# Value product of a pooled attention with 128-row operands in place of 48-row ones

## The chip, the cores and the metric

The kernel runs on one core of a Trainium2 chip. The metric is the device time of one execution in microseconds, from launch to end; the median of several runs stands for a kernel. One execution was recorded by the hardware profiler, and its span, from the first to the last instruction, is the profiled time.

## What is computed

An attention with pooled keys and values, and behind it two layers of a feed-forward network, in float32.

```python
# q, k, v: (8 batches, 8 heads, 576 tokens, 64)
k_p = k.reshape(B, H, 72, 8, D).mean(axis=3)      # 576 keys -> 72
v_p = v.reshape(B, H, 72, 8, D).mean(axis=3)
attn = softmax(q @ k_p.T / sqrt(D))
x = (attn @ v_p) as (4608 tokens, 512)
h = x @ moe_w_in;   x = piecewise(h) @ moe_w_out  # 512 -> 2048 -> 512
h = x @ moe2_w_in;  out = (h - tanh(h)) @ moe2_w_out
```

## The kernel before, in words

The 4608 tokens are cut into twelve blocks of 384 (`TB`). The first layer runs over all blocks, then the second, and each block takes 16 steps, one for each 128 of the 2048 inner features. A step `t` is twelve products of 384 columns (`h_mm`, the tile `ph`) and twelve for step `t - 2` (`out_mm`, tiles `po`). A float32 product of full accuracy is made of three products of two halves each: an operand is cut into `hi`, a `float32r` number, and `lo`, the rest.

The attention of block `j` runs between the steps of the block ahead of it, one pair of heads (`p`) in four steps. A pair of heads has 2 x 72 = 144 pooled keys: 128 of them, the main part, fill a tile's rows, and 16 are left over. These 16 make the 48 rows of this change: the value side `vr` has the `hi` values, then their `lo` part, then `hi` again, 16 rows each, and the attention side `ar` the matching rows, so that one product gives the three terms for the 16 keys.

Block 0's attention and the conversion of the first weights come ahead of the first step (`startup`); during the first 14 steps the weights of the first layer are converted from float64 on ScalarE, VectorE and GpSimd (`w1_prep`, `conv`). A table of step numbers (`plan`) says in which step each piece of attention is issued, and a scheduler in the building program then orders the instructions of each engine.

The functions that matter here:

- `constants` clears `kvraw`'s third part on GpSimd and makes the identity `ident`.
- `kv_pool` sums eight neighbouring keys and values on GpSimd into `bd`: `bd[:, 0]` and `bd[:, 1]` are the 128 main keys and values, `bd[:, 2]` the 16 left over, copied to several rows, the keys' at rows 64 to 79.
- `kv_v` (lines 224 to 234) makes `vh`, `vl` and the 48-row `vr` on VectorE. `vr` comes from a pool of five tiles.
- `kv_k_pe` (236 to 241) turns the keys on TensorE, the main ones by a 128-row transpose (`L239`), the 16 by a 16-row one (`L240`), into one PSUM tile `pkt`.
- `softmax_b` writes the normalised attention and takes a tile `ar` of 48 rows from a pool with one place; `at_pe` turns it; `at_evac` copies the result into `ar`, rows 0 to 31 on ScalarE, rows 32 to 47 on VectorE.
- `pv` (382 to 394) is the value product: four products into one PSUM tile, `vh`, `vl`, `vr`, `vh` against attention (`L390` to `L393`). A block that lies in two batches has two pieces of 192 columns, others one of 384.

Of the kernel before, what the change touches and what calls it, by code (L numbers as in the profile page):

```python
# [17 lines left out]

# Float32 products at float32 accuracy: every operand is cut exactly into
# hi = float32r(x) and lo = x - hi, and a*b is hi*hi + hi*lo + lo*hi.  # L20
#
# The weights come in as float64. A pair of 32-bit words becomes the nearest float32:
# taken as a float32, the upper word has the exponent's upper eight bits as its exponent,
# so that times 2**-112 moves the exponent's bias by 896, from float64's to float32's
# (what is too small becomes 0). The bits then move up by three, the lower word's upper
# three bits, rounded, are added, and the sign is put back.
REBIAS = 2.0**-112
# [3 lines left out]
def attention_two_moe_kernel(  # L31
# [11 lines left out]
    nc = tc.nc  # L43
# [34 lines left out]

# [1 line left out]
    kvraw = const.tile([P, 3, POOL * D], F32, tag="kvraw", name="kvraw")  # L80
    ident = const.tile([P, P], F32, tag="ident", name="ident")
    half = const.tile([P, 1], F32, tag="half", name="half")
    mask = const.tile([P, 2], F32, tag="mask", name="mask")
    nsel = const.tile([P, 1], F32, tag="nsel", name="nsel")

    def constants(sel):
        nc.gpsimd.memset(kvraw[:, 2, :], 0.0)
        make_identity(nc, ident)
        nc.vector.memset(half, 0.5)
        nc.vector.memset(nsel, 0.0)  # L90
        nc.vector.memset(nsel[32:48], -1.0)
        nc.vector.tensor_reduce(mask[:, 0:1], ident[:, 0:SP], AX.X, ALU.add)
        nc.vector.tensor_reduce(mask[:, 1:2], ident[:, SP:P], AX.X, ALU.add)
        nc.vector.tensor_scalar(mask, mask, 1.0 / POOL, None, ALU.mult)
        nc.vector.memset(sel, 0.0)
        nc.vector.tensor_scalar(sel[:, SP : 2 * SP], ident[0:SP, 0:SP], 1.0 / POOL, None, ALU.mult)
        for c in range(3):
            o = 3 * SP + c * NR
            nc.vector.tensor_scalar(sel[:, o : o + NR], ident[0:SP, SP - NR : SP], 1.0 / POOL, None, ALU.mult)

# [1 line left out]
    WI = [None] * FC  # L102
# [30 lines left out]
    def w1_prep(f):  # L133
        r = raws.pop((0, f))
        if f + 1 < FC - 1:
            # the room that the next weights will have
            a, s = w_slot(f + 1, "l", I32, "wf"), w_slot(f + 1, "h", I32, "ws")
        else:
            a, s = staging(), r[..., 0]
        conv(r, a, s)  # L140
        hi, lo = (w_slot(f, x, F32R, f"w{x}") for x in "hl")
        a = a.bitcast(F32)
        nc.scalar.activation(hi, a, AF.Copy)  # L143
        for io, eng in ((0, nc.vector), (1, nc.gpsimd)):
            eng.tensor_tensor(lo[:, io], a[:, io], hi[:, io].bitcast(F32), ALU.subtract)  # L145
            (WI, WO)[io][f] = (hi[:, io], lo[:, io])
# [16 lines left out]

# [1 line left out]
    xt = {}  # L165
# [21 lines left out]
    def pieces(j):  # L187
        """(first token in block, tokens, batch, first token in batch)"""
        done, res = 0, []
        while done < TB:  # L190
            b, s = divmod(j * TB + done, S)
            n = min(TB - done, S - s)
            res.append((done, n, b, s))
            done += n
        return res
# [8 lines left out]
    def tree(eng, a):  # L204
        """sums of the POOL parts of the last axis, left in its first part"""
        n = POOL * D // 2
# [4 lines left out]
    def kv_pool(b, p):  # L211
# [7 lines left out]
        eng.tensor_scalar(bd[:, 2, D : 2 * D], kvraw[:, 2, 0:D], 1.0 / POOL, None, ALU.mult)  # L219
        r = slice(HP, HP + NR)  # L220
        U[("k", b, p)] = (bd[:, 0], bd[r, 2], ident[r, r])
        U[("v", b, p)] = (bd[:, 1], bd[0:48, 2])

    def kv_v(b, p):
        main, rem = U.pop(("v", b, p))
        vh = kvp.tile([P, P], F32R, tag="vh", name="vh")
        vl = kvp.tile([P, P], F32R, tag="vl", name="vl")
        vr = kvp.tile([48, P], F32R, tag="vr", name="vr")
        vx = at.tile([48, P], F32R, tag="vx", name="vx")
        nc.vector.tensor_copy(vh, main)  # L230
        nc.vector.tensor_copy(vx, rem)
        nc.vector.tensor_tensor(vl, main, vh.bitcast(F32), ALU.subtract)
        nc.vector.scalar_tensor_tensor(vr, vx.bitcast(F32), nsel[0:48], rem, ALU.mult, ALU.add)
        vt[(b, p)] = (vh, vl, vr)

    def kv_k_pe(b, p):
        main, rem, idr = U.pop(("k", b, p))
        ps = ps_a.tile([P, 2 * SP], F32, tag="pa", name="pkt")
        nc.tensor.transpose(ps[:, 0:P], main, ident)  # L239
        nc.tensor.transpose(ps[:, P : 2 * SP], rem, idr)  # L240
        U[("pkt", b, p)] = ps
# [54 lines left out]
    def parts(j):  # L296
        """(batch, tile of tokens in the block, first token in the tile, tokens)"""
        if j == 1:
# [32 lines left out]
    def softmax_b(j, p, eng):  # L331
# [11 lines left out]
        if n == 3:  # L343
            eng.tensor_copy(rr[:, :, 2], px)
        ar = at.tile([48, TB], F32R, tag="ar", name="ar")
        U[("pr", j, p)] = (pn, rr, ar)

    def at_pe(j, p):
        pn, rr, ar = U.pop(("pr", j, p))
        pm = p_tile(j, [P, TB], "pam")  # L350
# [7 lines left out]
        else:  # L358
            pr = ps_a.tile([96, P], F32, tag="pa", name="par")
            nc.tensor.transpose(pr, rr.rearrange("t i c s -> t (i c s)").bitcast(F32), ident)  # L360
        U[("pm", j, p)] = (pm, pr, ar)

    def at_evac(j, p):
        pm, pr, ar = U.pop(("pm", j, p))
        ah = a_tile(j, [P, TB], F32R, "ah")
        al = a_tile(j, [P, TB], F32R, "al")
        if j < 2:
            nc.scalar.activation(ah, pm, AF.Copy)
            nc.vector.tensor_tensor(al, pm, ah.bitcast(F32), ALU.subtract)
            nc.scalar.activation(ar, pr, AF.Copy)  # L370
        else:
            for i in range(NTI):
                c = slice(i * P, (i + 1) * P)
                nc.scalar.activation(ar[0:32, c], pr[32 * i : 32 * i + 32], AF.Copy)
                nc.vector.tensor_copy(ar[32:48, c], pr[32 * i : 32 * i + NR])
            nc.scalar.activation(ah, pm, AF.Copy)
            nc.vector.tensor_tensor(al, pm, ah.bitcast(F32), ALU.subtract)
        U[("at", j, p)] = (ah, al, ar)

    def pv(j, p):  # L380
        ah, al, ar = U.pop(("at", j, p))
        ps = p_tile(j, [P, TB], "ppv")
        for off, n, b, s in pieces(j):
            vh, vl, vr = vt[(b, p)]
            if j == 1:
                t = slice(b * HP, (b + 1) * HP)
                o, xh, xr, xl = (x.rearrange("p (i t) -> p i t", t=P)[:, :, t] for x in (ps, ah, ar, al))
            else:
                o, xh, xr, xl = (x[:, off : off + n] for x in (ps, ah, ar, al))
            nc.tensor.matmul(o, vh, xh, start=True, stop=False)  # L390
# [10 lines left out]

# [1 line left out]
    hp = {}  # L403
# [93 lines left out]

# [1 line left out]
    def startup(used):  # L499
# [88 lines left out]

# [1 line left out]
    plan = {}  # L590
# [8 lines left out]
    def ahead(kind, fn, a):  # L599
        """Queue a load; each is issued when a buffer of its kind has been used."""  # L600
        loads[kind].append((fn, a))
# [119 lines left out]
```

## Time and profile before

| | us |
|---|---|
| median of 3 runs | 1824.53 |
| lowest, highest | 1823.83, 1825.07 |
| span of the profiled execution | 1822.8 |
| TensorE busy | 1782.7 (98%) |
| VectorE busy | 942.8 (52%) |
| ScalarE busy | 726.7 (40%) |
| GpSimd busy | 292.3 (16%) |

TensorE's products overlap: a product of 384 columns is shown as 0.34 us long while the next starts half that later. What it costs on the queue is therefore read from the distance of two starts. A float32 product that is no transpose is two passes in the trace, and each has a record of its own.

### The profile page before, as it was taken

The numbers are of one execution on the slowest core, as the hardware profiler recorded it, in microseconds if no ns is written. First come the engines' busy times: TensorE is split into PE (matmuls) and PEld (weight loads), VectorE is DVE, ScalarE is ACT, GpSimd is POOL, SyncE is SP. The second block draws the span as 40 slices with busy tenths as digits, with TensorE's granted clock in tenths as the row PEclk, the third lists the DMA queues.
The fourth block names the chain that finished last, engine by engine and source line by source line (L and its number), as shares of the span: only waits on it lengthen the run. The fifth ranks groups of instructions, "written<-read, shape, count | busy, mean of one in ns | idle before, by whom it ended". The sixth has DMA issues, their size and how long they took to land.

```text
span 1822.8 us, 25870 instructions
## 1 busy us (share of the span) xinstructions
PE 1782.7 (98%) x9616; PEld 1654.3 (91%) x9616; DVE 942.8 (52%) x1841; ACT 726.7 (40%) x1849; POOL 292.3 (16%) x382
## 2 busy tenths in 40 slices
PE   6888999999999999999999999999999999999999
PEld 4778999999999999999999999999999999999998
DVE  6898676766677666665556432332332332332222
ACT  4665554544444454443445432332232322332222
POOL 4695133320332202320100000000000000000000
PEclk8899999999999999999999999999999999999999
DMA  6462233413323232320114210110110010010000
GB/s 176 162 185 79 78 91 87 115 39 94 94 74 97 71 96 61 83 56 10 27 47 127 81 35 1 35 35 1 35 35 1 35 35 18 18 35 18 18 18 18
DMA packets 129133, 110.47 MB, mean 61 GB/s; under 512 B 71280, under 2 KB 102000, under 8 KB 129008
## 3 DMA queue, kind: packets, MB, share of 16 engines
q1 hardware_dynamic: 129008, 108.83, 20.0%
q8 instruction: 75, 1.23, 0.3%
q14 instruction: 50, 0.41, 0.1%
HBM read 81.53 MB, written 27.26 MB: 60 GB/s over the span
## 4 chain that ended last, share of the span: by engine, by line
PE 92%; DVE 3%; POOL 1%; DMA 1%; issue 1%; ACT 0%; SPq 0%; DVEq 0%; ACTq 0%; POOLq 0%
PE ph L416 43%; PE po L466 35%; PE pox L466 7%; PE psc L314 2%; PE ppv L392 1%; PE ppv L393 1%; DMA wraw<-in_moe_w_out_dram 1%; PE pam L352 1%; DVE ws L121 1%; PE ppv L390 0%; PE ppv L391 0%; DVE wl L145 0%; DMA kvs<-in_k_dram 0%; POOL wl L145 0%; POOL kvraw L208 0%
## 5 line engine op out<-in xcount | busy, mean ns | idle before, releaser
L416 PE MATMUL ph<-xh,wh 128*128 128x384 f32 x1536 | 524.3, 342 | 2.2 <-ACT wh L143 2.0
L416 PE MATMUL ph<-xh,wl 128*128 128x384 f32 x1536 | 519.3, 338 | 5.5 <-DVE wl L145 5.3
L416 PE MATMUL ph<-xl,wh 128*128 128x384 f32 x1536 | 517.5, 337 | 0.3 <-DVE xl L400 0.3
L433 DVE TENSOR_TENSOR g<-ph,g 128x384 f32<-128x384 f32 x384 | 213.5, 556 | 412.2 <-ACT g L427 315.5
L441 DVE TENSOR_TENSOR gl<-g,gh 128x384 fp32r<-128x384 f32 x369 | 233.7, 633 | 297.6 <-ACT gh L439 296.0
L439 ACT ACTIVATE gh<-g 128x384 fp32r<-128x384 f32 x384 | 200.9, 523 | 333.2 <-PE po L466 185.1
L416 PEld LDWEIGHTS ph<-xh,wh 128*128 128x128 f32 x1536 | 289.3, 188 | 13.7 <-ACT wh L143 2.6
L416 PEld LDWEIGHTS ph<-xl,wh 128*128 128x128 f32 x1536 | 290.0, 189 | 9.0 <-DVE xl L400 0.6
L416 PEld LDWEIGHTS ph<-xh,wl 128*128 128x128 f32 x1536 | 289.8, 189 | 7.7 <-DVE wl L145 7.6
L466 PE MATMUL po<-gh,wh 128*128 128x384 f32 x768 | 262.4, 342 | 0.0
L466 PE MATMUL po<-gl,wh 128*128 128x384 f32 x768 | 258.7, 337 | 1.9 <-POOL gl L441 1.9
L466 PE MATMUL po<-gh,wl 128*128 128x384 f32 x768 | 258.5, 337 | 0.0
L427 ACT ACTIVATE g<-ph 128x384 f32<-128x384 f32 x192 | 94.2, 491 | 325.8 <-PE ph L416 325.8
L425 ACT ACTIVATE g<-g,half 128x384 f32<-128x384 f32 x192 | 118.3, 616 | 163.8 <-DVE g L424 163.5
L466 PE MATMUL po<-wh,gl 128*128 128x512 f32 x384 | 151.9, 396 | 0.0
L466 PE MATMUL po<-wl,gh 128*128 128x512 f32 x384 | 151.7, 395 | 0.0
L466 PE MATMUL po<-wh,gh 128*128 128x512 f32 x384 | 150.3, 391 | 0.0
L466 PEld LDWEIGHTS po<-gl,wh 128*128 128x128 f32 x768 | 145.1, 189 | 2.8 <-POOL gl L441 2.8
L466 PEld LDWEIGHTS po<-gh,wl 128*128 128x128 f32 x768 | 145.1, 189 | 0.0
L466 PEld LDWEIGHTS po<-gh,wh 128*128 128x128 f32 x768 | 145.0, 189 | 0.0
L424 DVE TENSOR_SCALAR g<-ph 128x384 f32<-128x384 f32 x192 | 106.3, 554 | 65.2 <-PE ph L416 61.8
L208 POOL TENSOR_TENSOR kvraw<-kvraw 128x768 f32<-128x768 f32 (+2 forms) x84 | 108.2, 1288 | 109.8 <-DMA kvraw<-in_v_dram 89.4
(119 smaller groups left out, 1953.8 us busy)
## 6 DMA issues: line engine op xcount, KB each, us to landing
wraw<-in_moe_w_in_dram SPq DMA_DIRECT2D x32, 512.0 KB, 4.0
wraw<-in_moe_w_out_dram SPq DMA_DIRECT2D x32, 512.0 KB, 4.7
x2d<-ost SPq DMA_DIRECT2D x48, 192.0 KB, 1.9
xl<-x2d SPq DMA_DIRECT2D x12, 768.0 KB
out_dram<-ost SPq DMA_DIRECT2D x36, 256.0 KB, 2.0
w2d<-wf SPq DMA_DIRECT2D x32, 256.0 KB, 2.3
wl<-w2d SPq DMA_DIRECT2D x32, 256.0 KB, 2.6
kvraw<-in_k_dram SPq DMA_DIRECT2D x28, 256.0 KB, 2.7
```

Of the source, the lines that this page charges most:

```text
L121: nc.vector.scalar_tensor_tensor(s, hw, -0x80000000, s, ALU.bitwise_and, ALU.bitwise_or)
L208: eng.tensor_tensor(a[..., 0:n], a[..., 0:n], a[..., n : 2 * n], ALU.add)
L314: nc.tensor.matmul(ps[t : t + m, i], qt[:, c], kt[(b, p)], start=True, stop=True)
L352: nc.tensor.transpose(pm[:, i * P : (i + 1) * P], pn[:, i, 0:P], ident)
L416: nc.tensor.matmul(ps, a[:, cs], x[:, c, :], start=(i == 0), stop=(i == 3 * KC - 1))
L424: nc.vector.tensor_scalar(a, hp[t], -1.0, 1.0, ALU.max, ALU.min)
L425: nc.scalar.activation(a, a, AF.Square, bias=half, scale=0.5)
L427: nc.scalar.activation(a, hp[t], AF.Tanh)
L433: nc.vector.tensor_tensor(a, hp.pop(t), a, ALU.subtract if ph else ALU.max)
L439: nc.scalar.activation(gh, a, AF.Copy)
L441: eng.tensor_tensor(gl, a, gh.bitcast(F32), ALU.subtract)
L466: nc.tensor.matmul(o, a, m, start=(f == 0 and i == 0), stop=(f == FC - 1 and i == 2))
```

## The change

The tile `vr` becomes one of six tiles of 128 rows that live through the whole kernel, used in turn, and `ar` one of two such tiles, by the parity of `p`. All eight are cleared once on GpSimd in `constants`, and later writes touch rows 0 to 47 alone, so rows 48 to 127 stay zero. The third value product takes all 128 rows. The 16 left-over keys are no longer turned by a 16-row transpose: all 128 rows of `bd[:, 2]` stand as the stationary operand against 16 columns of the identity, those of rows 64 to 79, in an ordinary float32 product. Comments are dropped.

```diff
+    vrs = [const.tile([P, P], F32R, tag=f"vr{i}", name=f"vr{i}") for i in range(6)]
+    ars = [const.tile([P, TB], F32R, tag=f"ar{i}", name=f"ar{i}") for i in range(2)]
+    n_vr = itertools.count()
...
         nc.vector.memset(nsel[32:48], -1.0)
+        for t in (*vrs, *ars):
+            nc.gpsimd.memset(t.bitcast(F32), 0.0)
...
-        r = slice(HP, HP + NR)
-        U[("k", b, p)] = (bd[:, 0], bd[r, 2], ident[r, r])
+        U[("k", b, p)] = (bd[:, 0], bd[:, 2])
...
-        vr = kvp.tile([48, P], F32R, tag="vr", name="vr")
+        vr = vrs[next(n_vr) % len(vrs)]
...
-        nc.vector.scalar_tensor_tensor(vr, vx.bitcast(F32), nsel[0:48], rem, ALU.mult, ALU.add)
+        nc.vector.scalar_tensor_tensor(vr[0:48], vx.bitcast(F32), nsel[0:48], rem, ALU.mult, ALU.add)
...
-        nc.tensor.transpose(ps[:, P : 2 * SP], rem, idr)
+        nc.tensor.matmul(ps[:, P : 2 * SP], rem, ident[:, HP : HP + NR], start=True, stop=True)
...
-        ar = at.tile([48, TB], F32R, tag="ar", name="ar")
...
+        ar_t = ars[p % 2]
...
-            nc.scalar.activation(ar, pr, AF.Copy)
+            nc.scalar.activation(ar_t[0:48], pr, AF.Copy)
...
-                nc.scalar.activation(ar[0:32, c], pr[32 * i : 32 * i + 32], AF.Copy)
-                nc.vector.tensor_copy(ar[32:48, c], pr[32 * i : 32 * i + NR])
+                nc.scalar.activation(ar_t[0:32, c], pr[32 * i : 32 * i + 32], AF.Copy)
+                nc.vector.tensor_copy(ar_t[32:48, c], pr[32 * i : 32 * i + NR])
...
-                o, xh, xr, xl = (x[:, off : off + n] for x in (ps, ah, ar, al))
+                o, xh, xr, xl = (x[:, off : off + n] for x in (ps, ah, ar_t, al))
```

The scheduler orders the first part of the program anew. On GpSimd, at the very start, the program before clears `kvraw`, the identity and a part of `bd`, and goes on to the sums of block 0's values (`kvs`):

```order
L87 MEMSET kvraw 128x512
masks.py:197 MEMSET ident 128x128
L218 MEMSET bd 128x64
masks.py:199 ISA
masks.py:199 AFFINE_SELECT ident<-ident 128x128
L517 TENSOR_TENSOR kvs<-kvs 72x2x256
```

and now, on the same engine at the same place:

```order
masks.py:197 MEMSET ident 128x128
L99 MEMSET vr_130 128x128
masks.py:199 ISA
masks.py:199 AFFINE_SELECT ident<-ident 128x128
L99 MEMSET vr_131 128x128
L99 MEMSET vr_132 128x128
L99 MEMSET vr_133 128x128
L99 MEMSET vr_134 128x128
L99 MEMSET vr_135 128x128
L99 MEMSET ar_136 128x384
L99 MEMSET ar_137 128x384
L226 MEMSET bd 128x64
```

One of the eight new clearings stands ahead of the identity's last step, the other seven behind it and ahead of the first value sum.

On TensorE in block 0's attention (`pq` are the turned queries, `psc` the scores, `pv` the pooled values of the last head pairs) the order was:

```order
L314 MATMUL psc<-kt,qt 128x144 x3
L542 MATMUL pv_382<-vp,sel 128x64
L543 MATMUL pv_382<-vp,sel 48x64
L280 MATMUL pq_421<-ident,qn 64x128 x3
L278 MATMUL pq_421<-ident,qn 64x128 x3
L314 MATMUL psc<-kt,qt 128x144 x3
L390 MATMUL ppv<-ah,vh 128x384
L391 MATMUL ppv<-ah,vl 128x384
L392 MATMUL ppv<-ar,vr 128x384
L393 MATMUL ppv<-al,vh 128x384
```

and is now:

```order
L321 MATMUL psc<-kt,qt 128x144 x3
L550 MATMUL pv_394<-vp,sel 128x64
L551 MATMUL pv_394<-vp,sel 48x64
L398 MATMUL ppv<-ah,vh 128x384
L399 MATMUL ppv<-ah,vl 128x384
L400 MATMUL ppv<-ar_136,vr_130 128x384
L401 MATMUL ppv<-al,vh 128x384
L287 MATMUL pq_432<-ident,qn 64x128 x3
L285 MATMUL pq_432<-ident,qn 64x128 x3
L321 MATMUL psc<-kt,qt 128x144 x3
```

The first value product has moved ahead of the last pair's queries and scores.

On SyncE's queue, where batch 1's keys and values for the second head pair (`kvraw`) are loaded among the weights (`wraw`), the order was:

```order
L200 DMA kvraw<-in_k_dram 128x512
L202 DMA kvraw<-in_k_dram 16x512
L200 DMA kvraw<-in_v_dram 128x512
L110 DMA wraw<-in_moe_w_in_dram 128x4x256
L114 DMA wraw<-in_moe_w_out_dram 128x1024
L202 DMA kvraw<-in_v_dram 16x512
L110 DMA wraw<-in_moe_w_in_dram 128x4x256
L114 DMA wraw<-in_moe_w_out_dram 128x1024
L202 DMA kvraw<-in_v_dram 16x512 x2
```

and is now:

```order
L208 DMA kvraw<-in_k_dram 128x512
L210 DMA kvraw<-in_k_dram 16x512
L118 DMA wraw<-in_moe_w_in_dram 128x4x256
L122 DMA wraw<-in_moe_w_out_dram 128x1024
L208 DMA kvraw<-in_v_dram 128x512
L210 DMA kvraw<-in_v_dram 16x512
L118 DMA wraw<-in_moe_w_in_dram 128x4x256
L122 DMA wraw<-in_moe_w_out_dram 128x1024
L210 DMA kvraw<-in_v_dram 16x512 x2
```

The 128 main rows of the values went behind a pair of weight loads; the last two loads of the same tile stand where they stood.

## Rows read from the trace of the kernel before

**Rows 1.** Page, chain that ended last: share of the span by engine.

```profile
PE 92%; DVE 3%; POOL 1%; DMA 1%; issue 1%; ACT 0%; SPq 0%; DVEq 0%; ACTq 0%; POOLq 0%
```

**Rows 2.** Windows: busy us per engine (instructions), then granted TensorE clock, DMA share, GB/s.

```profile
40.00:60.00 20.00, 16.96 (x55) 12.55 (x55) 17.76 (x33) 10.26 (x19) 9.12 (x8) 0.59 0.40 136
0.00:156.00 156.00, 119.87 (x614) 98.37 (x615) 133.19 (x217) 94.36 (x210) 107.09 (x99) 0.92 0.53 161
156.00:960.00 804.00, 803.66 (x4645) 773.31 (x4645) 527.01 (x1115) 375.94 (x1131) 185.20 (x284) 1.00 0.25 72
```

**Rows 3.** Timeline of TensorE, block 3's last value product; start us, duration us.

```profile
312.00 0.34 PE L390 MATMUL ppv<-ah,vh 128*128 128x384 f32 x1
312.17 0.34 PE L391 MATMUL ppv<-ah,vl 128*128 128x384 f32 x1
312.44 0.44 PE L392 MATMUL ppv<-ar,vr 48*128 48x384 f32 x1
312.82 0.44 PE L393 MATMUL ppv<-al,vh 128*128 128x384 f32 x1
313.10 0.34 PE L466 MATMUL po<-gh,wh 128*128 128x384 f32 x1
...
315.01 0.34 PE L466 MATMUL po<-gh,wl 128*128 128x384 f32 x1
```

**Rows 4.** Timeline of TensorE, a value product in two pieces, block 1.

```profile
162.00 0.25 PE L390 MATMUL ppv<-ah,vh 128*128 128x192 f32 x1
162.09 0.28 PE L391 MATMUL ppv<-ah,vl 128*128 128x192 f32 x1
...
162.78 0.27 PE L390 MATMUL ppv<-ah,vh 128*128 128x192 f32 x1
162.89 0.27 PE L391 MATMUL ppv<-ah,vl 128*128 128x192 f32 x1
...
163.57 0.36 PE L466 MATMUL po<-gh,wh 128*128 128x384 f32 x1
```

**Rows 5.** Timeline of TensorE, transposes of the keys and what follows.

```profile
231.48 0.27 PE L239 MATMUL pkt<-ident,bd 128*128 128x128 f32 x1
231.68 0.23 PE L240 MATMUL pkt<-ident,bd 16*128 16x16 f32 x1
...
232.12 0.34 PE L416 MATMUL ph<-xl,wh 128*128 128x384 f32 x1
```

**Rows 6.** Timeline of TensorE, four full-height transposes between products.

```profile
306.75 0.34 PE L416 MATMUL ph<-xh,wl 128*128 128x384 f32 x1
306.93 0.49 PE L352 MATMUL pam<-ident,ex 128*128 128x128 f32 x3
...
307.54 0.34 PE L466 MATMUL po<-gl,wh 128*128 128x384 f32 x1
```

**Rows 7.** TensorE by line and form, 156:960 us: xcount, busy us, mean ns.

```profile
L392 PE MATMUL ppv<-ar,vr 48*128 48x384 f32 x28 | 12.4, 442 | 0.1
...
L392 PE MATMUL ppv<-ar,vr 48*128 48x192 f32 x26 | 9.2, 355 | 0.0
...
L240 PE MATMUL pkt<-ident,bd 16*128 16x16 f32 x24 | 5.5, 231 | 0.0
```

**Rows 8.** Timeline of TensorE, the scores' six float32 passes.

```profile
217.81 0.90 PE L314 MATMUL psc<-kt,qt 128*128 128x144 f32 x6
...
218.72 0.34 PE L416 MATMUL ph<-xl,wh 128*128 128x384 f32 x1
```

**Rows 9.** Timeline of GpSimd at the start.

```profile
1.18 0.20 POOL masks.py:197 MEMSET ident<- 128x128 f32 x1
...
17.09 2.06 POOL L517 TENSOR_TENSOR kvs<-kvs 72x512 f32<-72x512 f32 x2 [15.29 <-DMA kvs<-in_v_dram]
```

**Rows 10.** Chain in order of time, 40 to 112 us: start us, us, what.

```profile
56.75 3.52 PE ph L416 x10
...
104.52 7.29 DMA wraw<-in_moe_w_out_dram
```

More of the change, by code (lines that the diff above doesn't have):

```diff
@@ L1 @@
+import itertools
 from contextlib import ExitStack
@@ L232, in kv_v @@
         nc.vector.tensor_tensor(vl, main, vh.bitcast(F32), ALU.subtract)
-        nc.vector.scalar_tensor_tensor(vr, vx.bitcast(F32), nsel[0:48], rem, ALU.mult, ALU.add)
+        nc.vector.scalar_tensor_tensor(vr[0:48], vx.bitcast(F32), nsel[0:48], rem, ALU.mult, ALU.add)
         vt[(b, p)] = (vh, vl, vr)
     def kv_k_pe(b, p):
-        main, rem, idr = U.pop(("k", b, p))
+        main, rem = U.pop(("k", b, p))
         ps = ps_a.tile([P, 2 * SP], F32, tag="pa", name="pkt")
         nc.tensor.transpose(ps[:, 0:P], main, ident)
-        nc.tensor.transpose(ps[:, P : 2 * SP], rem, idr)
+        nc.tensor.matmul(ps[:, P : 2 * SP], rem, ident[:, HP : HP + NR], start=True, stop=True)
         U[("pkt", b, p)] = ps
@@ L344, in softmax_b @@
             eng.tensor_copy(rr[:, :, 2], px)
-        ar = at.tile([48, TB], F32R, tag="ar", name="ar")
-        U[("pr", j, p)] = (pn, rr, ar)
+        U[("pr", j, p)] = (pn, rr)
     def at_pe(j, p):
-        pn, rr, ar = U.pop(("pr", j, p))
+        pn, rr = U.pop(("pr", j, p))
         pm = p_tile(j, [P, TB], "pam")
@@ L360, in at_pe @@
             nc.tensor.transpose(pr, rr.rearrange("t i c s -> t (i c s)").bitcast(F32), ident)
-        U[("pm", j, p)] = (pm, pr, ar)
+        U[("pm", j, p)] = (pm, pr)
     def at_evac(j, p):
-        pm, pr, ar = U.pop(("pm", j, p))
+        pm, pr = U.pop(("pm", j, p))
+        ar_t = ars[p % 2]
         ah = a_tile(j, [P, TB], F32R, "ah")
@@ L373, in at_evac @@
                 c = slice(i * P, (i + 1) * P)
-                nc.scalar.activation(ar[0:32, c], pr[32 * i : 32 * i + 32], AF.Copy)
-                nc.vector.tensor_copy(ar[32:48, c], pr[32 * i : 32 * i + NR])
+                nc.scalar.activation(ar_t[0:32, c], pr[32 * i : 32 * i + 32], AF.Copy)
+                nc.vector.tensor_copy(ar_t[32:48, c], pr[32 * i : 32 * i + NR])
             nc.scalar.activation(ah, pm, AF.Copy)
             nc.vector.tensor_tensor(al, pm, ah.bitcast(F32), ALU.subtract)
-        U[("at", j, p)] = (ah, al, ar)
+        U[("at", j, p)] = (ah, al)
     def pv(j, p):
-        ah, al, ar = U.pop(("at", j, p))
+        ah, al = U.pop(("at", j, p))
+        ar_t = ars[p % 2]
         ps = p_tile(j, [P, TB], "ppv")
@@ L386, in pv @@
                 t = slice(b * HP, (b + 1) * HP)
-                o, xh, xr, xl = (x.rearrange("p (i t) -> p i t", t=P)[:, :, t] for x in (ps, ah, ar, al))
+                o, xh, xr, xl = (x.rearrange("p (i t) -> p i t", t=P)[:, :, t] for x in (ps, ah, ar_t, al))
             else:
-                o, xh, xr, xl = (x[:, off : off + n] for x in (ps, ah, ar, al))
+                o, xh, xr, xl = (x[:, off : off + n] for x in (ps, ah, ar_t, al))
             nc.tensor.matmul(o, vh, xh, start=True, stop=False)
```

## The prediction

> **What bounds the kernel now.** I read the chain of waits first: TensorE is 92% of it [rows 1]. The busy times by stretch then show two regimes [rows 2]. From 156 to 960 us TensorE is busy 803.66 of 804 us at granted clock 1.00, while VectorE has 527 of them, ScalarE 376 and GpSimd 185: every nanosecond taken off TensorE's queue there comes off the end. In the first 156 us it is busy 119.87 us only, VectorE 133.19 and GpSimd 107.09: there the preparation of weights sets the pace, and a faster product mostly ends in a later wait.
>
> Inside the long stretch the starts of TensorE's products show what this change touches. A 128-row product on 384 columns follows the one before by 0.17 us (312.00 to 312.17) [rows 3]. At the value product's third member, `L392`, whose operands have 48 rows, the step is 0.27; to the fourth, with 128 rows again, it is 0.38; to the next step's first product 0.28. From 312.00 to 313.10 the four take 1.10 us. Eleven undisturbed steps from there to 315.01 take 1.91, 0.174 each, and four of those would be 0.69. TensorE stands still by 0.41 us, in three pieces of about 0.10, 0.21 and 0.10. With two pieces of 192 columns the picture repeats [rows 4]: 128-row neighbours step by 0.09 (162.00 to 162.09) and 0.11 (162.78 to 162.89), but from 162.09 over the 48-row member to 162.78 three steps take 0.69, and the eight of the pair 1.57 up to 163.57. The 16-row transpose at `L240` shows it a third time [rows 5]: 0.20 from the full transpose to it, and 0.44 from there over the next step's first product to its second.
>
> Two readings compete: the gaps belong to the change of operand height, or to a wait of the instruction. The second fits badly. `L393` and the first product behind it have a gap each and carry no wait in the program's order, and in block 1, from which [rows 4] are, `L392` carries none either. Full-height transposes between two sorts of product leave no such gap: from 306.75 to 307.54 there lie one product, three transposes, a fourth and another product, 0.79 us in all, which is two steps of 0.17 and four of 0.11 [rows 6]. What a rule says to this: the Trainium skill, "TensorEngine Tiling (Array Packing)", section "Key Properties", says that changing the tiling mode drains the array; with the gaps at both edges of the 48 and 16 rows the trace agrees, and by it the full-height form has no drain left.
>
> **The change part by part.**
> *Value products.* From 156 us on there are 28 quads of 384 columns and 26 of 192, the latter in 13 pairs [rows 7]. A single goes from 1.10 to 0.69 us: 28 x 0.41 = 11.4 us. A pair's eight steps go from 1.57 to 0.09 + 7 x 0.11 = 0.86 us: 13 x 0.71 = 9.2 us. Together 20.6 us, all on the path. The stationary tile has 128 columns before and after and the moving one 384 or 192, so I charge no more for the larger height; the neighbours `L390` and `L391` with 128 rows are the price.
>
> *Last 16 keys.* The transpose of 16 rows becomes a float32 product, which the trace splits into two passes (the queries' product at `L314` has twice as many records as instructions). Passes like these cost (218.72 - 217.81 - 0.17) / 6 = 0.12 us with 144 columns [rows 8]; with 16 columns the load of 128 weight columns should bound them, as in the transposes' 0.11 [rows 6]. Now transpose plus `L240` cost 232.12 - 231.48 - 0.17 = 0.47 us [rows 5]; then 3 x 0.11 = 0.33. With 24 of them behind 156 us [rows 7] that is 24 x 0.14 = 3.3 us; I take 3.1, since no row has 16 columns against 128 rows. The bounds: if these gaps stay and the second pass is added, a loss of 24 x 0.12 = 2.9; at best the same 0.14, 3.4.
>
> *Clearing eight tiles on GpSimd.* Clearing 128x128 took 0.20 us [rows 9]; six of these are 1.2, and two of three times the width at three times the price 1.2 more. The order puts them between the identity and the first value sums, and GpSimd idles there for 15.29 us until the values land at 17.09 [rows 9]. Only the first cleared tile precedes the identity's last step, where a 128x64 clearing stood: the difference is under 0.1 us. Cost nothing; without that cover, 2.4.
>
> *Persistent tiles.* `vr` has six places for five, `ar` two for one. VectorE's write of `vr` no longer waits for TensorE to let the old tile go; nothing is queued behind a new wait. GpSimd's and ScalarE's work is otherwise the same in number. No gain: with TensorE full, nobody waited for these [rows 2].
>
> *Order of the start.* From its 281st row on TensorE's order is the same in both programs. Before that block 0's first value product moves ahead of the last head pair's query turns, and on SyncE a value load goes behind a pair of weight loads. TensorE is short of work there, so I take 0. The bounds: on the gain side the four quads and three pairs of the first 156 us, some of them at half clock (granted 0.59 from 40 to 60 us, [rows 2]): at most 4 x 0.41 x 2 + 3 x 0.71 = 5.4 us. On the loss side one weight load that comes a turn late; the longest on the chain of this stretch lasts 7.29 us [rows 10]. The value load that moves is covered, since the last part of the same tile stays behind the next pair of weight loads.
>
> **Sum.** 11.4 + 9.2 + 3.1 + 0 = 23.7 us. The profiled span is 1822.8, the median 1824.5; the 1.7 around the span stay. 1824.5 - 23.7 = **1800.8 us**.
>
> **The rivals.**
> *The gaps are not of the height.* If they belong to the operand's data or its writer, they stay and `L240` adds a pass: 1824.5 + 2.9 = 1827.4. For it speaks that `L392` does carry a wait from block 2 on; against it [rows 4 to 6]. Chance 0.05, of which I give 0.01 to slower by over 0.2%.
> *The load of the higher tile isn't hidden.* If the load of 128 rows of `vr` can't run under the product ahead, each of the 54 third members pays 0.11 again: 5.9 us, 1806.7. Against it: `L391` with 128 rows steps by 0.17 behind `L390`, its load hidden [rows 3]. Chance 0.04. This is what the Trainium skill, "TensorE: Matmul & The Clock Gate", Part 3, "The mechanism", says against the change: a load overlaps a running product only where the row groups differ. The trace contradicts it for 128-row neighbours.
> *The start loses more.* One to two weight loads late, 7 to 15 us: 1808 to 1816. For it speaks that VectorE is busy 133 of these 156 us [rows 2]; against it that only the order moved, not the work. Chance 0.09.
> *Slower than before: the clock of the start.* TensorE's clock is granted at 0.59 from 40 to 60 us, half of 2.4 GHz for most of it, and products cost 3.52 / 10 = 0.35 at its end [rows 10]. If the new order left it at that level further on, each us of work would cost a second. It decides once 23.7 us of work more than now run at half clock, at its worst, with all the 119.87 - 16.96 = 103 us of work outside 40 to 60 us [rows 2] in it, the run ends near 1904. Against it: the mean over the 156 us is 0.92 [rows 2], so the low level is soon left now, and fewer gaps make TensorE no idler. Chance 0.02.
>
> **How the numbers follow.** Forecast 0.80; the height rival 0.05, the load 0.04, the start 0.09, the clock 0.02. The forecast's own spread is -5.4 to +7.3 for the start and +6.0 if the 16-key gaps stay: 1795 to 1808 without the ends falling together. Taking in the load and half of the start's cases gives **1794 to 1811**. A change under 0.2% (3.6 us) can't be told from none. Faster 0.93, same 0.04, slower 0.03.
>
> **What would show it.** Right: behind 160 us the third and fourth value products step by 0.17 (or 0.11 with 192 columns), the quad ends 0.69 us after its start, transpose and both passes of the 16 keys take 0.33, and TensorE stays busy without a pause to the end. The clearing rows end before 6 us. Wrong: steps of 0.27 and 0.38 still stand behind 128-row operands; a new wait named at the product that reads `vr`; or the step at which TensorE becomes full moves from 156 us to 165 and later.

## The result, and the profile after

| | before | after |
|---|---|---|
| median of 4 runs each, us | 1824.18 | 1803.43 |
| lowest, highest | 1823.82, 1825.07 | 1801.40, 1804.23 |
| span of the profiled execution | 1822.8 | 1802.0 |
| TensorE busy | 1782.7 | 1759.1 |

The ratio of after to before is 0.9884, with a 95% interval from 0.987 to 0.9898: the change takes 20.75 us off. The prediction had 1800.8 us, 23.7 off, and its range was 1794 to 1811.

The kernel after, page, chain that ended last, as [rows 1]:

```profile
PE 92%; DVE 4%; POOL 2%; issue 1%; ACT 1%; DMA 0%; SPq 0%; DVEq 0%; POOLq 0%; ACTq 0%
```

The windows of the kernel after, in the columns of [rows 2]:

```profile
40.00:60.00 20.00, 15.06 (x77) 10.61 (x77) 19.18 (x38) 13.10 (x30) 12.44 (x9) 0.78 0.43 141
0.00:156.00 156.00, 118.98 (x620) 99.71 (x621) 134.66 (x220) 96.53 (x213) 115.84 (x108) 0.89 0.54 166
156.00:960.00 804.00, 802.32 (x4791) 793.34 (x4790) 534.69 (x1136) 386.13 (x1147) 181.16 (x283) 1.00 0.27 75
```

TensorE is still the chain, and from 156 to 960 us it is busy 802.32 of 804 us at clock 1.00. Beside [rows 2] that is 1.34 us less, the first sign of something that the prediction did not have.

TensorE's timeline after, start and duration in us: a single value product, which answers to [rows 3].

```profile
307.29 0.34 PE L398 MATMUL ppv<-ah,vh 128*128 128x384 f32 x1
307.46 0.34 PE L399 MATMUL ppv<-ah,vl 128*128 128x384 f32 x1
307.64 0.34 PE L400 MATMUL ppv<-ar,vr 128*128 128x384 f32 x1
307.81 0.34 PE L401 MATMUL ppv<-al,vh 128*128 128x384 f32 x1
307.99 0.34 PE L474 MATMUL po<-gh,wh 128*128 128x384 f32 x1
```

Every step is 0.17 or 0.18, and the four take 0.70 us where [rows 3] show 1.10. The same timeline at the fourth value product of block 1, a pair of pieces, and at a turn of the keys, for [rows 4] and [rows 5]:

```profile
161.26 0.25 PE L398 MATMUL ppv<-ah,vh 128*128 128x192 f32 x1
161.35 0.28 PE L399 MATMUL ppv<-ah,vl 128*128 128x192 f32 x1
...
162.13 0.36 PE L474 MATMUL po<-gh,wh 128*128 128x384 f32 x1
...
229.06 0.27 PE L246 MATMUL pkt<-ident,bd 128*128 128x128 f32 x1
229.16 0.29 PE L247 MATMUL pkt<-ident,bd 128*128 128x16 f32 x2
...
229.56 0.34 PE L424 MATMUL ph<-xl,wh 128*128 128x384 f32 x1
```

The pair's eight steps take 0.87 us instead of 1.57. From the full transpose to the second product behind it 0.50 pass; less one product's 0.17, transpose and two passes take 0.33 us instead of 0.47.

GpSimd's timeline at the start, beside [rows 9]:

```profile
1.80 0.79 POOL L99 MEMSET vr<- 128x128 f32 x5
2.53 0.78 POOL L99 MEMSET ar<- 128x384 f32 x2
...
15.73 2.07 POOL L525 TENSOR_TENSOR kvs<-kvs 72x512 f32<-72x512 f32 x2 [12.33 <-DMA kvs<-in_v_dram]
```

The clearing ends at 3.3 us and GpSimd then waits 12.33 us for the values: the new work is covered.

What the prediction did not have stands in TensorE's waits from 160 to 945 us (for whom, us in total, times, longest us) and in its timeline at the first of the two:

```profile
PE pkt L246 <- DVE al L384: 1.3, 2, 0.7
```

```profile
362.90 0.34 PE L474 MATMUL po<-gh,wl 128*128 128x384 f32 x1
363.96 0.33 PE L246 MATMUL pkt<-ident,bd 128*128 128x128 f32 x1 [0.72 <-DVE al L384]
```

The step from 362.90 to 363.96 is 1.06 us instead of 0.17. The keys' transpose `L246` needs a place in PSUM that the turned attention `pam` still holds, until VectorE has taken `al` from it (`L384`). TensorE's waits of the kernel before had no such line. A second kind shows at the second value product of the blocks 2, 5 and 8 (here block 2):

```profile
193.91 0.34 PE L399 MATMUL ppv<-ah,vl 128*128 128x384 f32 x1
194.29 0.45 PE L400 MATMUL ppv<-ar,vr 128*128 128x384 f32 x1
194.58 0.33 PE L401 MATMUL ppv<-al,vh 128*128 128x384 f32 x1
```

Here steps of 0.38 and 0.29 still stand behind 128-row operands. The waits of the weight loads name the reason, after (first line) and, alike, before (second):

```profile
PEld ppv L400 <- DVE ar L382: 1.1, 3, 0.4
```

```profile
PEld ppv L392 <- DVE ar L375: 1.1, 3, 0.4
```

In three value products `ar` comes late in both kernels; before, the gap of the short operand lay over most of that wait.

To place the rest I use three stretches of TensorE's order, which is the same in both from there on but for the second pass of the keys: up to the fourth value product of block 1 (start 162.00 before [rows 4], 161.26 after), from there to the first product behind the last value product, and the rest. The first product behind the last value product, before and after:

```profile
939.48 0.34 PE L466 MATMUL po<-gh,wh 128*128 128x384 f32 x1
```

```profile
918.15 0.34 PE L474 MATMUL po<-gh,wh 128*128 128x384 f32 x1
```

| us | before | after | gain |
|---|---|---|---|
| up to the fourth value product of block 1 | 162.00 | 161.26 | 0.74 |
| the stretch of the value products | 777.48 | 756.89 | 20.59 |
| behind it, to the end of the span | 883.36 | 883.81 | -0.45 |

Below, "the stretch" is always the middle row. In it, by the mean distances of starts in the two traces, 28 singles went from 1.112 to 0.740 (10.4 us), 13 pairs from 1.568 to 0.888 (8.8), 24 turns of keys from 0.476 to 0.347 (3.1): 22.3 us. The two waits at `L246` take 1.06 and 0.95 instead of 0.17 each, 1.7 us in all. 22.3 - 1.7 = 20.6, which is the stretch's gain.

### The profile page after: what moved, and what is told of

Its sections match the earlier page's. It is cut to its first block, busy times and chain, and to the rows that moved or that the text cites. A ratio compares the mean times of both kernels' runs of the same rounds, so it can differ in the third digit from the quotient of the medians.

```text
span 1802.0 us, 25940 instructions
## 1 busy us (share of the span) xinstructions
PE 1759.1 (98%) x9644; PEld 1654.3 (92%) x9644; DVE 937.1 (52%) x1841; ACT 728.1 (40%) x1849; POOL 297.0 (16%) x390
## 4 chain that ended last, share of the span: by engine, by line
PE 92%; DVE 4%; POOL 2%; issue 1%; ACT 1%; DMA 0%; SPq 0%; DVEq 0%; POOLq 0%; ACTq 0%
PE ph L424 43%; PE po L474 35%; PE pox L474 7%; PE psc L321 2%; PE pam L358 1%; POOL wl L153 1%; PE ppv L400 1%; PE ppv L398 0%; PE ppv L401 0%; PE ppv L399 0%; DVE wl L153 0%; DVE wf L130 0%; DMA kvs<-in_k_dram 0%; DVE ws L129 0%; DVE wf L131 0%
## 5 line engine op out<-in xcount | busy, mean ns | idle before, releaser
L449 DVE TENSOR_TENSOR gl<-g,gh 128x384 fp32r<-128x384 f32 x369 | 228.3, 619 | 283.9 <-ACT gh L447 281.7
L333 ACT ACTIVATE ex<-psc,nm 128x72 f32<-128x72 f32 x288 | 89.4, 325 | 89.0 <-DVE nm L329 79.5
```

What stands on the lines that cost most here:

```text
L333: nc.scalar.activation(ex[:, g, :], ps[:, g, :], AF.Exp, bias=nm[:, g : g + 1], scale=scale, accum_out=sm[:, g : g + 1])
L449: eng.tensor_tensor(gl, a, gh.bitcast(F32), ALU.subtract)
```

## The experiments

The theory: a product whose operands have fewer rows than its neighbours' costs TensorE a gap at each change of height, and the change is worth the sum of these gaps. Rivals: the gain comes with the persistent tiles (a place that is free earlier, a wait gone) and not with the height; the load of the higher tile costs something; the start's new order makes the gain. For the shortfall of 3 us: the waits at `L246` come from VectorE, which GpSimd slows, against the form of the keys' product. Times of runs are medians, ratios are to the kernel before in the same group of runs.

### The parts one by one

Values alone: the kernel after, with the 16-row transpose of the keys back.

```diff
-        U[("k", b, p)] = (bd[:, 0], bd[:, 2])
+        r = slice(HP, HP + NR)
+        U[("k", b, p)] = (bd[:, 0], bd[r, 2], ident[r, r])
...
-        nc.tensor.matmul(ps[:, P : 2 * SP], rem, ident[:, HP : HP + NR], start=True, stop=True)
+        nc.tensor.transpose(ps[:, P : 2 * SP], rem, idr)
```

> The changed kernel with the 16-row transpose of the last keys put back; the value products keep their 128 rows. Order of TensorE, GpSimd and SyncE as in the changed kernel. Height theory (TensorE stands still at each edge between 128-row operands and shorter ones): the gaps of 0.20 and 0.16 + 0.10 us around the 16-row transpose come back in 24 places behind 156 us, +3.3 us on the changed kernel: 1805.5 to 1808. Rival (the 16 keys' gaps are none of the height, the product in two passes costs as much): 1802 to 1804.

Keys alone: the kernel before, with the 128-row product for the 16 keys.

```diff
-        U[("k", b, p)] = (bd[:, 0], bd[r, 2], ident[r, r])
+        U[("k", b, p)] = (bd[:, 0], bd[:, 2])
...
-        nc.tensor.transpose(ps[:, P : 2 * SP], rem, idr)
+        nc.tensor.matmul(ps[:, P : 2 * SP], rem, ident[:, HP : HP + NR], start=True, stop=True)
```

> The kernel before with the keys' part alone: the last 16 keys by a 128-row product with 16 identity columns, the value products with 48 rows as before. TensorE's and GpSimd's order as before. Height theory: transpose and both passes take 0.33 us in place of 0.47, 24 times: 1824.2 - 3.3 = 1821 (1819.5 to 1822.5). Rival (the gaps stay and a pass of 0.12 us is added): 1827.

| | us | ratio, 95% | the stretch |
|---|---|---|---|
| values alone | 1807.71 | 0.9915 (0.9901 to 0.9928) | 760.91 |
| keys alone | 1820.47 | 0.9983 (0.9975 to 0.9992) | 774.19 |

The keys alone take 3.29 us off the stretch, without a wait of TensorE for another engine in it. The values alone take 16.57, and three waits at the keys' transpose stand in that kernel, the longest here (timeline of TensorE):

```profile
595.58 0.33 PE L247 MATMUL pkt<-ident,bd 128*128 128x128 f32 x1 [1.57 <-DVE al L385]
```

So the waits do not come with the new form of the keys' product. Since the kernel with 48 rows below has the same order of GpSimd and no such wait, they come with the shorter value products. The parts add up to 19.86 of the 20.59; the waits at the keys are 2.04 us in the values alone and 1.33 after, which is the rest.

### Height against the tiles that live through the kernel

The kernel after, persistent tiles, clearing, order of every engine and all, in which the third product reads 48, 64 or 96 of the 128 rows; the edit for 48, the others with 64 and 96 in its place:

```diff
-            nc.tensor.matmul(o, vr, xr, start=False, stop=False)
+            nc.tensor.matmul(o, vr[0:48], xr[0:48], start=False, stop=False)
```

> The changed kernel with its eight persistent tiles, its clearing, its keys' product and its order on every engine, but the third value product takes rows 0 to 47 alone. Height theory: the steps of 0.27, 0.38 and 0.28 us come back, 28 x 0.41 + 13 x 0.71 = 20.6 us less some 0.7 us of waits for the attention tile that the gaps cover: 1822 to 1825. Rival (the gain is that of the longer-lived tiles or of the new order of the start): 1802 to 1806.

> The changed kernel, order on every engine as there, but the third value product takes rows 0 to 63 of the same zero-padded tiles. Height theory, any operand short of the full array costs the two edges: as with 48 rows, 1822 to 1825, steps of 0.27, 0.38, 0.28. Rival (the cost lies in the 48 rows as such, say in their not filling a 64-row half): 1803, steps of 0.17.

> As the run with 64 rows, but rows 0 to 95. If every height other than 128 costs the edges: 1822 to 1825. If only the halves and quarters of the array do, and 96 rows run as the full height: 1803, steps of 0.17. The transpose of 96 columns in the kernel before says nothing on it, since there the rows were 128. I hold the second for likelier.

| rows read | us | ratio, 95% | the stretch |
|---|---|---|---|
| 48 | 1824.39 | 0.9998 (0.9989 to 1.0007) | 774.14 |
| 64 | 1823.18 | 0.9994 (0.9984 to 1.0004) | 774.14 |
| 96 | 1804.47 | 0.9892 (0.9875 to 0.9909) | 756.84 |
| 128 (after) | 1803.43 | 0.9884 (0.987 to 0.9898) | 756.89 |

With 48 rows the stretch is that of the keys alone, 774.14 against 774.19: what is left of the change without the height is, there, the keys' part. The timelines of TensorE, with 64 and with 96 rows:

```profile
312.84 0.34 PE L399 MATMUL ppv<-ah,vl 128*128 128x384 f32 x1
313.11 0.44 PE L400 MATMUL ppv<-ar,vr 64*128 64x384 f32 x1
313.49 0.44 PE L401 MATMUL ppv<-al,vh 128*128 128x384 f32 x1
313.76 0.34 PE L474 MATMUL po<-gh,wh 128*128 128x384 f32 x1
```

```profile
309.82 0.34 PE L399 MATMUL ppv<-ah,vl 128*128 128x384 f32 x1
310.00 0.34 PE L400 MATMUL ppv<-ar,vr 96*128 96x384 f32 x1
310.18 0.34 PE L401 MATMUL ppv<-al,vh 128*128 128x384 f32 x1
310.36 0.34 PE L474 MATMUL po<-gh,wh 128*128 128x384 f32 x1
```

64 rows have the steps of 48, 0.27, 0.38 and 0.27; 96 rows run in steps of 0.18 like 128. So the price does not grow with the missing rows, it is there or not there. The Trainium skill, "TensorEngine Tiling (Array Packing)", section "Available Configurations", knows heights of 32, 64 and 128 rows; 48 like 64 and 96 like 128 fit it if a height counts as the next larger of these, which the page does not say.

These four kernels have the same order on every engine, and the fourth value product of block 1 starts at 165.51, 163.38, 163.53 and 161.26 us. Kernels with the same gaps (48 and 64 rows, 96 and 128 rows) differ by 2.1 and 2.3 us there: a start that differs by 2 us between two profiles proves nothing.

By the whole time the kernel with 48 rows is slower than the keys alone, with equal stretches: its ten runs lie from 1820.62 to 1825.24 us, the eleven of the keys alone from 1819.43 to 1822.66, and the medians are 3.9 apart; the runs with 64 rows lie from 1822.77 to 1824.35. In the profiles 0.4 us of it lies behind the stretch and the rest ahead of it: the stretch starts at 165.51 (in the slowest of the ten runs) and 160.87 us, and the mean granted clock over the first 160 us is 0.86 and 0.90. So the persistent tiles, their clearing and the new order of the start together seem to cost some us of the start in the kernels with short rows; which of the three does it, no run separates.

### One edge or one product: two short products side by side

The kernel before, where a pair's eight products are ordered so that its two 48-row ones are neighbours.

```diff
+        todo = []
...
-            nc.tensor.matmul(o, vh, xh, start=True, stop=False)
-            nc.tensor.matmul(o, vl, xh, start=False, stop=False)
-            nc.tensor.matmul(o, vr, xr, start=False, stop=False)
-            nc.tensor.matmul(o, vh, xl, start=False, stop=True)
+            todo.append(((vh, xh), (vl, xh), (vr, xr), (vh, xl), o))
+        seq = [(k, i) for m in ((0, 1), (2,), (3,)) for k in range(len(todo)) for i in m]
+        for n, (k, i) in enumerate(seq):
+            nc.tensor.matmul(todo[k][4], *todo[k][i], start=(n == 0), stop=(n == len(seq) - 1))
```

> The kernel before, but where a block lies in two batches the two 48-row products stand side by side, so that a pair has one way into the short height and one out in place of two. Theory of the edges: the pair's excess of 0.71 us halves, 13 x 0.36 = 4.6 us less, 1819 to 1821 (the single ones stay). Rival (each short product costs by itself, or the one behind it): 1824, no change.

```profile
329.52 0.27 PE L394 MATMUL ppv<-ah,vl 128*128 128x192 f32 x1
329.73 0.47 PE L394 MATMUL ppv<-ar,vr 48*128 48x192 f32 x2
330.12 0.47 PE L394 MATMUL ppv<-al,vh 128*128 128x192 f32 x2
330.43 0.36 PE L467 MATMUL po<-gh,wh 128*128 128x384 f32 x1
```

The pair, which starts at 329.21, now takes 1.22 us instead of 1.57: one short product's gap of the two is gone (0.35). The gap belongs to the change of height, not to a product or its operand. The run took 1818.63 us, ratio 0.9976 (0.9963 to 0.9988). The stretch gained 2.64 of the 13 x 0.35 = 4.6 us. Most of the other 1.9 went into new waits: a first-layer product waits for VectorE's `xl` (0.65 us), two of the pairs take 0.33 longer each than the rest, and this row:

```profile
193.51 0.44 PE L394 MATMUL ppv<-ar,vr 48*128 48x384 f32 x1 [0.34 <-DVE ar L375]
```

So here, too, part of a gain on TensorE returns as a wait for VectorE.

### The keys cheaper still, earlier, later

One pass: all 128 rows of `bd[:, 2]` are turned by a full transpose, which is one pass, into columns 64 to 191; the main keys then overwrite the columns up to 127, and the 16 wanted ones stand at 128 to 143, the last that the copy out of PSUM takes.

```diff
-        ps = ps_a.tile([P, 2 * SP], F32, tag="pa", name="pkt")
+        ps = ps_a.tile([P, P + HP], F32, tag="pa", name="pkt")
+        nc.tensor.transpose(ps[:, HP : HP + P], rem, ident)
         nc.tensor.transpose(ps[:, 0:P], main, ident)
-        nc.tensor.matmul(ps[:, P : 2 * SP], rem, ident[:, HP : HP + NR], start=True, stop=True)
...
-        nc.scalar.activation(t, ps, AF.Copy)
+        nc.scalar.activation(t, ps[:, 0 : 2 * SP], AF.Copy)
```

> The changed kernel with the last 16 keys by one full transpose of all 128 rows, into columns 64 to 191 of the PSUM tile, ahead of the main transpose that then writes over columns 0 to 127; the 16 wanted columns come to stand at 128 to 143 as before. One pass of 0.11 us less in 24 places: -2.6 us, 1799.5 to 1802 if the start and the two stalls of the changed kernel at the keys' transpose (0.7 and 0.6 us, waiting for VectorE) stay as they are. Rival (the two passes run under something else already): 1803.4, no change.

```profile
322.33 0.27 PE L246 MATMUL pkt<-ident,bd 128*128 128x128 f32 x1
322.44 0.27 PE L247 MATMUL pkt<-ident,bd 128*128 128x128 f32 x1
...
322.72 0.34 PE L424 MATMUL ph<-xl,wh 128*128 128x384 f32 x1
...
495.90 0.30 PE L246 MATMUL pkt<-ident,bd 128*128 128x128 f32 x1 [1.36 <-DVE al L384]
```

A turn of the keys costs 0.39 - 0.17 = 0.22 us instead of 0.33, 24 x 0.11 = 2.6 us in all, and the stretch has 756.86 against 756.89: nothing. The waits at `L246` grew to three, 0.48, 1.36 and 0.75 us. Time 1804.98, ratio 0.9896 (0.9882 to 0.991).

Earlier: from block 2 on GpSimd's sums, the keys' turn and its copy out of PSUM (`kv_k_evac`) come one step ahead.

```diff
-                add(st - 1, "pool", kv_pool, b, p)
+                add(st - 1 - (j > 1), "pool", kv_pool, b, p)
...
-                add(st, "pe1", kv_k_pe, b, p)
-                add(st, "ev1", kv_k_evac, b, p)
+                add(st - (j > 1), "pe1", kv_k_pe, b, p)
+                add(st - (j > 1), "ev1", kv_k_evac, b, p)
```

> The changed kernel with the keys' transpose, product and evacuation of blocks 2 to 11 one step earlier, ahead of the attention's transposes rather than behind them, so that they need not wait for the PSUM place that VectorE frees with the subtraction al. Theory that part of the shortfall is these two waits (0.7 and 0.6 us, and 0.3 to 0.4 around them): they go, 156 to 960 us 1.5 to 2 us shorter, 1801.5. Rival (the wait moves to the attention's transposes, which then need the place that the keys hold): 1803.4 or more.

The waits at `L246` were gone, and the run took 1812.1 us, ratio 0.9935 (0.9919 to 0.9951). The stretch is 764.47 us, 7.58 longer than after, and five waits for `ar` in it take 7.38. The timelines of TensorE, VectorE and GpSimd at the longest show where it comes from:

```profile
275.57 0.44 PE L400 MATMUL ppv<-ar,vr 128*128 128x384 f32 x1 [3.06 <-DVE ar L382]
```

```profile
271.67 2.27 DVE L131 CUSTOM_DVE_ANT_0 wf<-wraw,wf 128x1024 uint16<-128x1024 uint16 x1
273.86 1.34 DVE L449 TENSOR_TENSOR gl<-g,gh 128x384 fp32r<-128x384 f32 x1
```

```profile
271.57 4.08 POOL L216 TENSOR_TENSOR kvraw<-kvraw 128x768 f32<-128x768 f32 x3 [5.03 <-DMA kvraw<-in_v_dram]
```

While GpSimd sums, two steps on VectorE, a weight conversion and `gl`, take 3.6 us, and `ar` stands behind them in VectorE's queue (it starts at 275.23). The keys' step was off the path; the moved sums made something else late.

Later: the keys' turn one step on, behind the value product.

```diff
-                add(st, "pe1", kv_k_pe, b, p)
-                add(st, "ev1", kv_k_evac, b, p)
+                add(st + (j > 1), "pe0" if j > 1 else "pe1", kv_k_pe, b, p)
+                add(st + (j > 1), "ev" if j > 1 else "ev1", kv_k_evac, b, p)
```

> The changed kernel with the keys' transpose, product and evacuation of blocks 2 to 11 half a step later: behind the value product instead of ahead of it, still ahead of the scores that read them. By then VectorE's subtraction al and the copies of the attention are long done. Theory (two waits at the keys' transpose for the PSUM place cost 1.8 us): they go, and no new wait comes, since two scores' steps are 2 us behind: 156 to 960 us 1.5 us shorter, 1801.5 to 1802. Rival (the wait moves to the scores, which now need the place that the keys' evacuation frees, or VectorE is late for the next reader instead): 1803 or more.

Again the waits at `L246` are gone, and the stretch has 757.16, no gain: six value products now wait for `ar`, 0.24 to 0.38 us each. Time 1805.07, ratio 0.989 (0.9875 to 0.9905). With the edit of the one-pass form on top of this one:

> As the run before, with the last 16 keys in one full transpose: 24 x 0.11 = 2.6 us less again, 1799. Rival (waits for VectorE grow by what TensorE saves, as when the one pass stood alone, 1805.0 with stalls of 2.6 us): 1801.5 to 1803.

The stretch is 754.99 (2.17 of the 2.6 us are kept now), the time 1801.35, ratio 0.9873 (0.9852 to 0.9895).

### Is it GpSimd that makes VectorE late?

VectorE and GpSimd, timelines of the kernel after, around the wait at 363.96:

```profile
361.64 1.33 DVE L449 TENSOR_TENSOR gl<-g,gh 128x384 fp32r<-128x384 f32 x1 [0.65 <-ACT gh L447]
...
363.37 0.54 DVE L384 TENSOR_TENSOR al<-pam,ah 128x384 fp32r<-128x384 f32 x1
```

```profile
359.63 3.80 POOL L216 TENSOR_TENSOR kvraw<-kvraw 128x768 f32<-128x768 f32 x3
```

`al` stands behind `gl`, with one step of 0.55 us between them, and `gl`, under the sums, takes 1.33 us. In the kernel before, the same `gl` took 0.72:

```profile
366.34 0.72 DVE L441 TENSOR_TENSOR gl<-g,gh 128x384 fp32r<-128x384 f32 x1 [0.65 <-ACT gh L439]
```

The scheduler's new order is not confined to the first part of the program. After the first 170 us GpSimd's order differs at two places, and these are the places of the two waits: before, the sums stood among the last steps of the softmax (`ex`, `rr`) and began 5 us ahead of `gl`; after, they stand in one piece behind those steps and begin 2 us ahead of it. GpSimd's timeline before:

```profile
361.39 1.85 POOL L208 TENSOR_TENSOR kvraw<-kvraw 128x768 f32<-128x768 f32 x1 [4.61 <-DMA kvraw<-in_v_dram]
363.64 1.06 POOL L336 TENSOR_TENSOR ex<-ex,rc 128x432 f32<-128x432 f32 x1 [0.40 <-DVE rc L335]
```

That order is not enough for a wait. With 48 rows and the new order VectorE's timeline has the same slow `gl`, and `al` is done at 371.59, while the keys' transpose is reached at 372.33:

```profile
369.32 1.33 DVE L449 TENSOR_TENSOR gl<-g,gh 128x384 fp32r<-128x384 f32 x1 [0.65 <-ACT gh L447]
```

No run has 128 rows with GpSimd's order of before, so whether the order is needed for the waits is not shown.

The test leaves out GpSimd's first and longest addition for the batches from 2 on (`cut` is `b > 1`), which shortens the sums and leaves every other engine its order.

```diff
-        n = POOL * D // 2
+        n = POOL * D // (4 if cut else 2)
...
-        tree(eng, kvraw)
+        tree(eng, kvraw, b > 1)
```

> The changed kernel with GpSimd's sums of keys and values cut short for batches 2 to 7: the first of the three additions is left out, so only half of each group of eight is summed. Order on TensorE, VectorE, ScalarE and SyncE as in the changed kernel, GpSimd as there but for four rows. Theory (VectorE is late at the two stalls since GpSimd's sums run at the same time and its 128x384 subtraction gl takes 1.33 us there instead of 0.56 to 0.72): the stalls go, the stretch from the fourth value product of block 1 to the last is 755.1 us instead of 756.9. Rival (VectorE is late by its own queue): the stalls stay at 0.6 to 0.7 us, 756.9.

```profile
359.17 0.56 DVE L449 TENSOR_TENSOR gl<-g,gh 128x384 fp32r<-128x384 f32 x1 [0.66 <-ACT gh L447]
```

`gl` takes 0.56, both waits at `L246` are gone, and the stretch has 754.85 us, 2.04 less than after, of which the waits were 1.7. The time is 1800.14, ratio 0.9863 (0.9848 to 0.9878). The three late `ar` stay. So, in the new order, the two waits are GpSimd's sums, by way of VectorE's `gl`. The Trainium skill, "SBUF — State Buffer", section "Who interferes with whom", says that a VectorE step with both inputs in SBUF, as `gl` has, contends with a GpSimd step that reads SBUF; 0.56 without and 1.33 with the sums agree.

### A faster version

From the late `ar` follows an order: the product that reads `ar` goes last of the four. On top of the later, one-pass keys:

```diff
-            nc.tensor.matmul(o, vr, xr, start=False, stop=False)
-            nc.tensor.matmul(o, vh, xl, start=False, stop=True)
+            nc.tensor.matmul(o, vh, xl, start=False, stop=False)
+            nc.tensor.matmul(o, vr, xr, start=False, stop=True)
```

> The kernel with the keys behind the value product and the last 16 in one transpose (1801.35 us), with the product that reads the tiles vr and ar as the last of the four instead of the third. Theory: its six waits for VectorE's last copy into ar (0.24 to 0.40 us) lose one step of 0.17 us each, 1.0 us together: 754.0 us from the fourth value product of block 1 to the last, 1800 to 1801 in all. Rival (the scheduler's new order of VectorE puts the copy later again): 1802 or more.

```profile
265.62 0.34 PE L400 MATMUL ppv<-al,vh 128*128 128x384 f32 x1
266.04 0.44 PE L401 MATMUL ppv<-ar,vr 128*128 128x384 f32 x1
```

Where `ar` is late the step is 0.42 instead of 0.58 (269.91 to 270.49 in the version before it), since a full product now lies ahead of it. TensorE has no wait left in the list of the stretch, which is 752.25 us, 2.74 less than in the version before it. The value products account for it: by the mean distances of starts singles went from 0.805 to 0.752 and pairs from 0.972 to 0.884, 28 x 0.053 + 13 x 0.088 = 2.6, more than the 1.0 expected. The median is 1796.58 (1795.38 to 1797.88), ratio 0.9845 (0.983 to 0.986), whose interval ends below that of after: this is faster than both kernels, by 28.2 us than before (1824.77 in the same group). Its profiled start, 157.98, was the earliest of all; since starts scatter by 2 us and more, no cause is given for that.

## Why the prediction was right, and where it was short

**The bound** held: TensorE sets the time from 156 us on, and what is taken off its queue there comes off the end, as long as nothing is waited for.

**The gaps are of the height.** Shown, from three sides: the same tiles with 48 rows bring the keys' part alone (774.14), 96 rows bring all (756.84), and two short products side by side cost one gap. The rivals fall with it: persistent tiles by themselves are worth nothing in the stretch (774.14 against 774.19), and outside it they bring no gain (0.9998 in all against 0.9983 for the keys alone); and the load of 128 rows is hidden (steps of 0.17 and 0.18 at `L400`). The Trainium skill, "TensorE: Matmul & The Clock Gate", Part 3, "The mechanism", lists a load as overlapping only where row groups differ, though a sentence ahead of that list also lets a load into the background weight buffer run ahead; these steps contradict the list for neighbours of full height.

**Sizes.** Singles 11.4 predicted, 10.4 measured; pairs 9.2 and 8.8; keys 3.1 and 3.1, with 3.3 when alone. The single's price was right for 25 of 28 (1.10 to 0.70, 0.01 above the 0.69 taken from longer rows); in the other three `L400` waits for `ar`, and they gain 0.19 instead of 0.4, 0.6 us in all. The price taken from one undisturbed row was multiplied by 28, though three of the 28 stood otherwise in the trace of before already (1.19 to 1.22 us).

**The step that failed** is "TensorE stays busy without a pause to the end". Two waits at the keys' transpose take 1.7 us. The prediction said of the persistent tiles that nothing is queued behind a new wait, and it asked of no other place what is late next. That GpSimd's work is "otherwise the same in number" was true, but in the two places its sums stood elsewhere in its order. With [rows 2] showing VectorE busy 527 of 804 us it seemed to have time to spare; but it has none for the 1 to 2 us in which `gl` runs under GpSimd's sums. In the kernel with the same orders and 48 rows, the keys' transpose comes later and finds `al` done: there is no such wait in its stretch. The gaps had been VectorE's time. How large such waits get was not to be had from the busy shares; which ones come could have been asked from the order (the sums beside `gl`, then `al`, then the keys' place in PSUM).

**The start** was put at 0 within -5.4 to +7.3. It gained 0.74 in the profiled pair, less than the 2 us by which kernels of the same order and gaps differ there. That it came out near 0 is probably in part luck: with 48 rows the new start lost some 3.5 us by the medians, and the faster products of the start, for which the prediction had up to 5.4 us, may have given it back; no run separates the two. Granted clock 0.78 against 0.59 from 40 to 60 us [rows 2] and 0.89 against 0.92 over the first 156 us show the low level (1.2 GHz) at another time and a little longer. The rivals "the start loses more" and "the clock of the start" did not come in the size that they had been given. **The clearing** was free, as said.

**Left open**: the last 0.45 us. Behind the last value product all starts of TensorE lie at the same distances before and after; its last product ends 3.71 us ahead of the end of the span before and 4.16 after. The difference stands in the closing step (`DRAIN`) of GpSimd at the program's end, which ends 0.45 us later. Before and seven kernels of the experiments have 883.3 to 883.4 us behind the last value product, after and the other five 883.75 to 883.85; why that step is late in these six, the runs do not show. Forecast and result then differ so: singles 1.0, pairs 0.4, waits at the keys 1.7, end 0.45, less the 0.74 of the start, is 2.8; 23.7 - 2.8 = 20.9, the difference of the spans (1822.84 and 1801.96).

## What to carry to other kernels

In a full stream of 128-row products one of 64 rows or fewer is paid for at each change of height: pad it to 128 rows with zeros that are written once, or set short ones side by side. When the full engine gets faster, compare the order of every engine and list who delivers to it in the next microsecond and what runs beside them; busy shares don't show it, the queue ahead of each deliverer does. The product that needs the latest operand goes last.

## What the runs showed of the hardware

- The price of a short operand does not follow its missing rows: 96 rows cost nothing, 64 cost as much as 48 (1.10 us for a quad of 384 columns in place of 0.70).
- With 16 columns, each of two float32 passes over 128 rows costs about 0.11 us, like a full transpose of 128 columns in one pass.
- A `gl` of VectorE takes 0.56 us alone and 1.33 under GpSimd's sums; a weight conversion (`L131`) took 0.69 at 194.26 in after and the 2.27 shown above beside the sums.
- Runs of one kernel scatter: the four of after lie 2.8 us apart, those of before 1.3 in the same group and 7.9 in a group of 21, and the profiled starts of kernels with the same order and gaps differ by 2.1 and 2.3 us.
